# First token chunk of a windowed-attention and SwiGLU kernel: normalising and turning it tile by tile instead of all four tiles together, with the first weight block holding both halves of its unit

## The chip, the cores and the metric

One core of a Trainium2 chip. The metric is device time in microseconds (us). Before the change it is 870.95 us, the median of three runs (868.99 to 872.09).

## The reference

The input is one sequence of 2048 tokens with 512 features. It is normalised without gain or bias; the result feeds both a windowed attention (32 heads of 16, each token sees itself and the 255 before it) and a SwiGLU network with 1792 hidden features. The network's output, passed through another silu, gates the attention's output, and the input is added.

```python
x = A_x
xn = _layernorm(x, axis=-1)             # (x - mean) / sqrt(var + 1e-5)
s = _A_ref(xn, A_wqkv, A_wo)            # q,k,v = xn @ wqkv; window 256; softmax; @ wo
g = _silu(_B_ref(xn, B_w_gate, B_w_up, B_w_down))   # (silu(xn@wg) * (xn@wu)) @ wd
return x + s * g
```

All is float32. A product of two float32 matrices is made here of three products of rounded parts: high with high, high with low and low with high.

## The kernel before, in words

**Tiling.** The tokens are cut into four chunks of 512, a chunk into four tiles of 128. A tile `xt` arrives with tokens on the partitions, is normalised in place, and is turned by TensorE (transposing matmuls against `ident`) into PSUM banks `xp_0` to `xp_3`, one bank for each 128 features, with 512 tokens along it. From each bank ScalarE writes the rounded part `xh`, and VectorE the rest, `xl = xp - xh`. These two are what the matmuls read.

**Weights.** A unit of dense work (`a` for the q and k projections, `g` and `u` for gate and up, `vp`, `d`, `s`) has a weight tile of 128 rows and up to 1024 columns. TensorE is used as two halves of 64 rows that work at the same time: half 0 takes rows 0 to 63 of a unit, half 1 rows 64 to 127, some time later and into the same PSUM bank. Weights therefore travel in blocks: block j holds the lower 64 rows of unit j and the upper 64 rows of unit j-1 (`w_fetch`). A block `wr` is fetched by two DMAs, ScalarE writes its rounded part `wh`, and GpSimd the rest `wl`, in pieces of 512 columns (`w_split`). Unit 0 is `a`, items `a_0` and `a_1`; unit 1 is the first `g` and `u`. So half 0 of `a` reads block 0, and half 1 reads block 1.

**Order.** The whole program is written out by a planner in Python that runs before the chip does anything. It keeps a clock of its own, `now`, and for each engine a queue of operations with a ready time, a slack and an assumed cost (`do`, `dma`); whatever is ready first by these numbers is emitted next. On the chip each engine then takes its instructions strictly in the emitted order and waits on semaphores where data are missing. A wrong assumed cost therefore changes no result, only the order. `next_mm` emits one matmul of one half; `ready` says when a half may go on; due times of the attention's matmuls go by dense work done (`work`), not by time.

**The start.** `load_x(0)` issues the four tile loads, two on SyncE and two on ScalarE. For each tile that lands VectorE runs `stats` (L256 and L257). After the fourth, `first_chain` (L260 to L283) makes the reciprocal root for all four tiles with thirteen small VectorE operations, then VectorE scales the four tiles (L291), and `x_turn` transposes each (L351). After the last tile `x_split` emits the four `xh` (L344) and four `xl` (L335) of 512 tokens. Meanwhile TensorE is given work on a constant tile, `warm_up` (L236): 20 matmuls of 128x128 at the start, 13 that wait for tile 3 to land, and 6 behind the last transposes. The first unit's item 0 takes its twelve 512-column matmuls of half 0 (L463), high parts of `x` first; then half 0 goes on with `a_1`, and half 1 begins `a_0`.

Of the kernel before, what the change touches and what calls it, by code (L numbers as in the profile page):

```python
# [55 lines left out]
def tile_window_attention_swiglu_gate(  # L56
# [181 lines left out]
    def load_x(c):  # L238
# [4 lines left out]
        left = [4]  # L243


        lnb = []
        if c == 0:
            lnb.extend(bank(rb_free, "ln"))
            ve, tm, r1 = (lnb[0][:, 4 * n : 4 * n + 4] for n in range(3))
            hv, t1 = (pers.tile([P, 4], F32, name=n) for n in ("hv", "t1"))  # L250

        def stats(i):
            st = sb(f"st{c}_{i}", [P, 6], F32, "st", 2)
            if c == 0 and i == 3:
                warm_up(xt[c, i][:, :P], 13)
            nc.vector.bn_stats(st, xt[c, i])  # L256
            nc.vector.bn_aggr(mv[:, i, :], st)  # L257

        def eps():
            nc.vector.tensor_scalar(ve, mv[:, :, 1], EPS, None, op0=ALU.add)  # L260

        def root():
            nc.gpsimd.tensor_scalar(ve, mv[:, :, 1], EPS, None, op0=ALU.add)
            nc.gpsimd.tensor_tensor(rs, ve, power[:, :4], op=ALU.pow)
            nc.gpsimd.tensor_tensor(tm, mv[:, :, 0], rs, op=ALU.mult)
            nc.gpsimd.tensor_scalar(tm, tm, -1.0, None, op0=ALU.mult)

        def roots(r=rs):

            i32 = mybir.dt.int32  # L270
            nc.vector.tensor_scalar(tm.bitcast(i32), ve.bitcast(i32), 1, None, op0=ALU.logical_shift_right)
            nc.vector.tensor_scalar(
                r.bitcast(i32), tm.bitcast(i32), -1, 0x5F3759DF, op0=ALU.mult, op1=ALU.add
            )

        def first_chain():
            eps()
            nc.vector.tensor_scalar(hv, ve, -0.5, None, op0=ALU.mult)
            roots(r1)
            for n in range(3):  # L280
                nc.vector.tensor_tensor(t1, r1, hv, op=ALU.mult)
                nc.vector.tensor_tensor(t1, r1, t1, op=ALU.mult)
                nc.vector.scalar_tensor_tensor(rs if n == 2 else r1, t1, 1.5, r1, op0=ALU.add, op1=ALU.mult)  # L283

        def scale(i):
            if c and i % 2 == 0:
                nc.scalar.activation(
                    xt[c, i], xt[c, i], AF.Identity, bias=tm[:, i : i + 1], scale=rs[:, i : i + 1]
                )
                return  # L290
            (nc.gpsimd if c else nc.vector).tensor_scalar(  # L291
                xt[c, i], xt[c, i], mv[:, i, 0:1], rs[:, i : i + 1], op0=ALU.subtract, op1=ALU.mult
            )
# [7 lines left out]

        def after_stats(t):
            left[0] -= 1
            if left[0] == 0 and c:
                do("G", t, 1.9, root, after_newton, sl)
            elif left[0] == 0:
                do("V", t, 2.5, first_chain, after_chain, -1.0)

        def after_chain(t):
            rb_free[lnb[1]] = t  # L310
            after_newton(t)

        def after_newton(t):
            for i in range(4):
                e = "SG"[i % 2] if c else "V"
                do(e, t, {"G": 2.1, "S": 0.62, "V": 0.55}[e], lambda i=i: scale(i), lambda t, i=i: scaled(t, i), sl + 0.3 * i)

# [5 lines left out]
        for i in range(4):  # L323
            dma(now[0], lambda i=i: fetch(i), lambda t, i=i: do("V", t, 0.8, lambda: stats(i), after_stats, sl),
                slack=0.1 * i, can=room(1) if c == 0 else room(5 - i + SPARE), e="S" if c == 0 and i % 2 else "D")

    xhigh = {}
    turned = []

    def x_split(c, k, pb, t, free):  # L330
        hi, lo = (xn[c % 2][s][:, k, :] for s in range(2))

        def low(t):
            xhigh[c, k] = t
            do("V", t, 0.61, lambda: nc.vector.tensor_tensor(lo, pb, f32(hi), op=ALU.subtract), done, -1.0)  # L335

        def done(t):
            free(t)
            xready[c, k] = t
            if k == KC - 1:  # L340
                for i in range(4):
                    give(xt.pop((c, i)))

        do("S", t, 0.52, lambda: nc.scalar.activation(hi, pb, AF.Copy), low, -2.0)  # L344


    def x_turn(i):
        if i == 0:
            turned.extend((bank(p, f"xp0_{k}"), p) for k, p in enumerate((rb_free, rb_free, fb_free, fb_free)))
        for k in range(KC):  # L350
            nc.tensor.matmul(  # L351
                turned[k][0][0][:, i * P : (i + 1) * P], xt[0, i][:, k * P : (k + 1) * P], ident,
                is_transpose=True, start=True, stop=True,
            )
# [16 lines left out]
    def latest(times):  # L371
        times = list(times)
        return None if any(t is None for t in times) else max(times)

    class Unit:
        src = None
        width = 0

        def wts(self, r):
            return wtile[self.n + r]  # L380

# [7 lines left out]
    ended_unit = {}  # L389

    def w_fetch(j):
        lo, up = weighted.get(j), weighted.get(j - 1)
        if lo is None and up is None:
# [4 lines left out]
        def go(r, u):  # L398
            if not box:
                box.append(sb(f"wr{j}", [P, 1024], F32, "wr", 2))  # L400
            move(box[0][half(r), : u.width], u.src[half(r)])
# [6 lines left out]
        for n, (r, u) in enumerate(parts):  # L408
            dma(now[0], lambda r=r, u=u: go(r, u), lambda t, n=n: then(t, n == len(parts) - 1),
                slack=1.0)  # L410

    def w_split(j):
# [3 lines left out]
        t = max(t, ended_unit.get(j - 3, 0.0))  # L416
        w = [weighted[i].width if i in weighted else 0 for i in (j, j - 1)]
        hi, lo = [], []
# [13 lines left out]

        def low(pr, a, b):
            nc.gpsimd.tensor_tensor(lo[0][pr, a:b], raw[pr, a:b], f32(hi[0][pr, a:b]), op=ALU.subtract)  # L434

        def done(t):
            left[0] -= 1
            if left[0] == 0:
                wready[j] = t
                timer(t - 0.5, w_fetch, j + 2)  # L440

        for n, (pr, a, b) in enumerate(cuts):
            sl = (0.0 if j >= 3 else 0.2) + 0.3 * n
            do("S", t, 0.13 + 0.00078 * (b - a), lambda pr=pr, a=a, b=b: high(pr, a, b),
               lambda t, pr=pr, a=a, b=b, sl=sl: do(
                   "G", t, 0.17 + 0.0021 * (b - a), lambda: low(pr, a, b), done, sl), sl)

# [4 lines left out]
    def unit_end(j, t):  # L452
        if (0, j) in half_ended and (j == 0 or (1, j - 1) in half_ended):
            ended_unit[j] = t
            w_split(j + 3)
# [51 lines left out]
    class Stationary(Unit):  # L507
# [11 lines left out]
        def mms(self, i, r, pb):  # L519
            w = [t.rearrange("p (a k n) -> p a k n", a=2, k=KC) for t in self.wts(r)]  # L520
            xs = xn[self.c % 2]
            steps = [(k, a, b) for k in range(KC) for a, b in PAIRS]
            first_unit = self.c == 0 and self.n == 0 and i == 0
            if first_unit:
                steps.sort(key=lambda o: o[2])
            for k, a, b in steps:
                def go(first, last, k=k, a=a, b=b):
                    return mm(pb, w[a][half(r), i, k, :], xs[b][half(r), k, :], first, last)
                if first_unit:
                    yield 512, go, lambda k=k, b=b: (xready if b else xhigh).get((0, k))  # L530
                else:
                    yield 512, go
# [769 lines left out]
    def next_mm(r):  # L1302
# [34 lines left out]
        else:  # L1337
            tag = tags.pop(n)
            if u.src is not None and i == 1:
                half_ended.add((1, u.n))  # L1340
                unit_end(u.n + 1, t)
            u.done(i, banks.pop(n), t, lambda t: fb_free.__setitem__(tag, t))


    def ready(r):
# [8 lines left out]
        if r == 0:  # L1354
            need = [bank_time(fb_free), u.inputs(i)]
            if u.src is not None:
                need.append(wready.get(u.n))
            return latest(need)
# [3 lines left out]
        if u.src is not None:  # L1362
            need.append(wready.get(u.n + 1))
        t = latest(need)
# [5 lines left out]

    xstart = [True]
    load_x(0)
    th0 = pers.tile([P, 1], F32, name="th0")
# [12 lines left out]
    while True:  # L1386
# [84 lines left out]
```

## Time and profile before

| | |
|---|---|
| median of three runs | 870.95 us |
| the profiled execution | 871.37 us |
| its span, first to last instruction | 869.7 us |
| what lies around the span | 1.67 us |
| TensorE busy in the span | 859.5 us (99%) |
| granted TensorE clock, mean | 0.999 |
| last `stats` ends | 8.15 us |
| root ends, scaling begins | 10.6 us |
| last transposes begin | 13.84 us |
| first real matmul (`a_0`, half 0) | 15.77 us |
| `a_1` of half 0 begins | 18.68 us |
| `a_0` of half 1 begins | 19.09 us |

Times inside the span count from its start. In a timeline row the columns are start, length, engine, line, operation, output and inputs, and a count. One 128x128 float32 matmul of the program leaves two records: 20 warm-up matmuls are a row with x40. A row that is merged shows the time from the first record's start to the last one's end. In a table of groups the two numbers behind the bar are the busy time and the mean length of one in ns.

### The profile page before, as it was taken

How to read it: one execution, taken by the hardware profiler on the slowest of the kernel's cores; microseconds unless marked ns; L12 is line 12 of the kernel's file. 1: busy time of each engine (PE TensorE's matmuls, PEld its weight loads, DVE VectorE, ACT ScalarE, POOL GpSimd, SP SyncE). 2: the span in 40 equal slices, each digit the busy share in tenths (PEclk: the TensorE clock that was granted, in tenths of full speed). 3: DMA queues.
4: the chain of work that ended last, by engine and by line, in shares of the span. 5: the costliest groups of instructions: out<-in, count | busy, mean ns of one | idle time of the engine just before them, and what ended most of it. 6: DMA issues, size and time to landing. Idle time of an engine off the chain costs nothing.

```text
span 869.7 us, 30126 instructions
## 1 busy us (share of the span) xinstructions
PE 859.5 (99%) x11966; PEld 798.1 (92%) x11966; DVE 499.1 (57%) x1650; ACT 489.9 (56%) x1046; POOL 627.4 (72%) x871
## 2 busy tenths in 40 slices
PE   9999999999999999999999999999999999999997
PEld 8899889899889998999999999899999999999897
DVE  5364466654765565766576666566555765554234
ACT  3345565555666466655566556655656665666431
POOL 5556587667777778767696798676768688869771
PEclk9999999999999999999999999999999999999999
DMA  5765846567676984766677987546666779644352
GB/s 148 187 167 121 221 115 168 126 162 167 148 198 180 251 201 105 152 156 133 155 184 194 214 200 181 129 145 151 158 150 173 174 187 209 162 130 112 108 126 74
DMA packets 69488, 139.62 MB, mean 161 GB/s; under 512 B 14546, under 2 KB 23250, under 8 KB 69348
## 3 DMA queue, kind: packets, MB, share of 16 engines
q1 hardware_dynamic: 69060, 137.18, 64.1%
q8 instruction: 94, 1.54, 0.8%
q10 hardware_dynamic: 288, 0.52, 0.2%
q14 instruction: 46, 0.38, 0.2%
HBM read 107.74 MB, written 29.62 MB: 158 GB/s over the span
## 4 chain that ended last, share of the span: by engine, by line
PE 93%; DMA 3%; DVE 1%; SPq 1%; POOL 0%; issue 0%; ACT 0%; ACTq 0%; DVEq 0%; POOLq 0%
PE u L463 18%; PE d L463 18%; PE g L463 17%; PE a L463 11%; PE pv L1148 8%; PE s L463 6%; PE c L1111 5%; PE vp L463 5%; PE b L960 4%; DMA q<-ms 1%; DMA r<-rd 1%; DMA xt<-x 1%; SPq L95 1%; DVE xt L291 0%; PE xp L481 0%
## 5 line engine op out<-in xcount | busy, mean ns | idle before, releaser
L434 POOL TENSOR_TENSOR wl<-wr,wh 128x512 fp32r<-128x512 f32 (+3 forms) x258 | 306.8, 1208 | 89.4 <-ACT wh L431 86.9
L968 DVE CUSTOM_DVE_ANT_0 jk<-b,maskb 128x384 bf16<-128x384 f32 (+2 forms) x512 | 271.5, 530 | 130.1 <-PE b L960 64.5
L1072 ACT ACTIVATE p<-c 128x384 f32<-128x384 f32 (+1 forms) x480 | 208.8, 489 | 127.1 <-PE c L1111 106.5
L463 PE MATMUL d<-wh,hh 64*128 64x256 f32 x1792 | 258.2, 278 | 0.0
L463 PEld LDWEIGHTS d<-wh,hh 64*128 64x128 f32 x1792 | 222.9, 185 | 1.0 <-issue 0.6
L463 PE MATMUL d<-wl,hh 64*128 64x256 f32 x896 | 201.3, 277 | 0.0
L431 ACT ACTIVATE wh<-wr 128x512 fp32r<-128x512 f32 (+3 forms) x258 | 142.2, 593 | 51.2 <-PE d L463 11.1
L463 PE MATMUL u<-xh,wh 64*128 64x512 f32 x448 | 167.3, 396 | 0.0
L463 PE MATMUL g<-xh,wh 64*128 64x512 f32 x448 | 167.2, 396 | 0.0
L463 PE MATMUL u<-xl,wh 64*128 64x512 f32 x448 | 166.9, 396 | 0.0
L463 PE MATMUL u<-xh,wl 64*128 64x512 f32 x448 | 166.9, 396 | 0.0
L463 PE MATMUL g<-xl,wh 64*128 64x512 f32 x448 | 166.5, 395 | 0.0
L463 PE MATMUL g<-xh,wl 64*128 64x512 f32 x448 | 164.8, 394 | 0.0
L1085 POOL TENSOR_SCALAR_AFFINE_SELECT p<-p 128x256 f32<-128x256 f32 x256 | 103.7, 410 | 77.1 <-ACT p L1072 75.6
L463 PEld LDWEIGHTS d<-wl,hh 64*128 64x128 f32 x896 | 144.4, 185 | 0.3
L960 PE MATMUL b<-k,q 48*128 48x384 f32 (+1 forms) x512 | 119.2, 333 | 0.0
L1111 PE MATMUL c<-q,k 49*128 49x384 f32 (+1 forms) x704 | 115.5, 302 | 2.3 <-DMA q<-ms 1.2
L1089 POOL TENSOR_SCALAR_AFFINE_SELECT p<-p 128x256 f32<-128x256 f32 x224 | 91.6, 410 | 13.2 <-ACT p L1072 13.1
L463 PE MATMUL a<-xh,wh 64*128 64x512 f32 x256 | 97.2, 394 | 0.0
L463 PE MATMUL a<-xh,wl 64*128 64x512 f32 x256 | 96.4, 392 | 0.0
L616 POOL TENSOR_TENSOR hh<-h,hh 128x512 fp32r<-128x512 f32 x56 | 72.5, 1295 | 33.0 <-ACT hh L612 32.7
L463 PE MATMUL a<-xl,wh 64*128 64x512 f32 x256 | 96.2, 393 | 0.0
(109 smaller groups left out, 2096.6 us busy)
## 6 DMA issues: line engine op xcount, KB each, us to landing
wr<-wgu SPq DMA_DIRECT2D x112, 256.0 KB
k<-qkd SPq DMA_DIRECT2D x48, 192.0 KB
wr<-wqk SPq DMA_DIRECT2D x32, 256.0 KB
qkd<-qkh SPq DMA_DIRECT2D x32, 256.0 KB
qkd<-qkl SPq DMA_DIRECT2D x32, 256.0 KB
q<-qkd SPq DMA_DIRECT2D x64, 128.0 KB
wr<-wdn SPq DMA_DIRECT2D x32, 256.0 KB
od<-ev SPq DMA_DIRECT2D x32, 256.0 KB
```

Source lines behind the costliest of these rows:

```text
L95: eng.dma_start(dst, src)
L431: nc.scalar.activation(hi[0][pr, a:b], raw[pr, a:b], AF.Copy)
L434: nc.gpsimd.tensor_tensor(lo[0][pr, a:b], raw[pr, a:b], f32(hi[0][pr, a:b]), op=ALU.subtract)
L463: return nc.tensor.matmul(pb, a, b, start=first, stop=last, skip_group_check=True)
L616: nc.gpsimd.tensor_tensor(hl[:, 1, :], self.h, f32(hl[:, 0, :]), op=ALU.subtract)
L960: nc.tensor.matmul(pb[:, :w], qs[u % 3][r : r + 48, p, qb * P : (qb + 1) * P], ks[u % 3][r : r + 48, p, lo : lo + w], start=True, stop=True,)
L968: nc.vector.tensor_tensor_reduce(junk[:, :n], pb[:, :n], maskb[:, 3 * P - n :], 1.0, -3.0e38, ALU.add, ALU.max, m[:, col : col + 1],)
L1072: nc.scalar.activation(t[:, h, :], pc[:, a:b], AF.Exp, scale=DH ** -0.5)
L1085: nc.gpsimd.affine_select(s, s, [[0, 2], [1, P]], ALU.is_ge, 0.0, base=0, channel_multiplier=-1)
L1089: nc.gpsimd.affine_select(s, s, [[0, 2], [-1, P]], ALU.is_gt, 0.0, base=0, channel_multiplier=1)
L1111: nc.tensor.matmul(pc[:, at0 : at0 + w], ks[u % 3][r : r + 49, p, k0 : k0 + P], qs[u % 3][r : r + 49, p, qb * P : qb * P + w], start=(i == ...
L1148: nc.tensor.matmul(pbs[r][0][32 * j : 32 * j + 32, q0:q1], vt[half(r), (4 * c + kb) % VT, VW * (4 * g + j) : VW * (4 * g + j) + 32], t[hal ...
```

## The change

Only the first chunk and the first three weight blocks are touched directly.

- Root and scaling go tile by tile. After a tile's `stats`, GpSimd runs `root(i, i + 1)`: add, power, and for the first two tiles also the product `-mean * rs`. The tiles that come first and second are scaled by ScalarE, the third and fourth by VectorE. `first_chain` is gone.
- A tile is turned as soon as it is scaled. When two tiles (256 tokens) are turned, `x_split` emits `xh` and `xl` for that part: eight of each with 256 tokens instead of four with 512.
- Half 0 and half 1 of `a_0` run as 24 matmuls of 256 columns each, in the order high-high, low weights, low `x`, and within each first part 0, then part 1. They may begin when their own part and their own 512 columns of the weight block are there (`wpart`).
- Block 0 holds both halves of unit 0; block 1 holds only the lower half of unit 1; block 2 is as before. `wready` and `unit_end` follow (`block`, `units_of`). Block 2 is fetched at planner time 8.5 into a buffer of its own.
- Block 0's first `wh` piece is pulled ahead (slack -3.0); GpSimd's `wl` waits until all four tiles are normalised, by a one-column copy into `spare`.
- Warm-up: 14 matmuls at the start; then, as long as the start lasts and no tile is ready by the planner's clock, the main loop emits one more and moves its clock on by 0.2133, or by 0.1117 once past 6.9. The 13 and the 6 are gone.

The core of the diff:

```diff
+        def root(a, b):
+            nc.gpsimd.tensor_scalar(ve[:, a:b], mv[:, a:b, 1], EPS, None, op0=ALU.add)
+            nc.gpsimd.tensor_tensor(rs[:, a:b], ve[:, a:b], power[:, a:b], op=ALU.pow)
+            if c == 0 and side(a) == "S":
+                nc.gpsimd.tensor_scalar(
+                    tm[:, a:b], mv[:, a, 0:1], rs[:, a:b], -1.0, op0=ALU.mult, op1=ALU.mult
+                )
...
+        def side(i):
+            return "SG"[i % 2] if c else "SSVV"[came.index(i)]
...
-        if i == 3:
-            warm_up(warm, 6)
-            xstart[0] = False
+        seen.add(i)
+        part = i // 2
+        if {2 * part, 2 * part + 1} <= seen:
             for k in range(KC):
                 (pb, tag), p = turned[k]
-                x_split(0, k, pb, now[0] + 0.2, lambda t, p=p, tag=tag: p.__setitem__(tag, t))
+                x_split(k, part, pb, now[0] + 0.2, lambda t, p=p, tag=tag: p.__setitem__(tag, t))
+        if len(seen) == 4:
+            xstart[0] = False
...
+    def block(n, r):
+        return n + r if n else 0
...
+    def units_of(j):
+        return weighted.get(j), weighted.get(j - 1 if j else 0) if j != 1 else None
...
+            if self.c == 0 and self.n == 0 and i == 0:
+                for a, b in ((0, 0), (1, 0), (0, 1)):
+                    for part in range(2):
+                        n = slice(256 * part, 256 * part + 256)
+                        for k in range(KC):
+                            def go(first, last, k=k, a=a, b=b, n=n):
+                                return mm(pb[:, n], w[a][half(r), i, k, :], xs[b][half(r), k, n], first, last)
...
-    warm_up(warm, 20)
+    warm_up(warm, 14)
...
     timer(7.0, w_fetch, 1)
+    timer(8.5, w_fetch, 2)
...
+        if xstart[0] and now[0] >= 4.1:
+            warm_up(warm, 1)
+            advance(0.2133 if now[0] < 6.9 else 0.1117)
+            continue
```

What the planner makes of it shows in the emitted order. First TensorE at the start, before the change; `xp_k<-ident,xt_i` is the transpose of feature group k of tile i, `[waits ...]` names the engine or DMA lane whose semaphore the instruction waits for.

```order
L236 MATMUL warm<-warm 128x128 x19
L236 MATMUL warm<-xt_3_139,warm 128x128 [waits DMAHW2_49]
L236 MATMUL warm<-xt_3_139,warm 128x128 x12
L351 MATMUL xp_0_206<-ident,xt_0_137 128x128 [waits DVE_49,Pool_49]
...
L351 MATMUL xp_0_206<-ident,xt_3_139 128x128 [waits DVE_49]
...
L351 MATMUL xp_3_209<-ident,xt_3_139 128x128
L236 MATMUL warm<-warm 128x128 x6
L463 MATMUL a_0_244<-xh_79,wh_194 128x512 [waits Activation_49]
```

The same place after the change, from the first matmul to the first ones of `a_1`:

```order
L236 MATMUL warm<-warm 128x128 x36
L338 MATMUL xp_0_191<-ident,xt_1_127 128x128 [waits Activation_49]
...
L236 MATMUL warm<-warm 128x128 x8
L338 MATMUL xp_0_191<-ident,xt_0_129 128x128 [waits Activation_49]
...
L338 MATMUL xp_0_191<-ident,xt_3_131 128x128 [waits DVE_49]
...
L236 MATMUL warm<-warm 128x128
L338 MATMUL xp_0_191<-ident,xt_2_133 128x128 [waits DVE_49,Activation_49]
...
L467 MATMUL a_0_239<-xh_79,wl_220 128x256 [waits Pool_49]
L467 MATMUL a_0_239<-xl_80,wh_219 128x256 [waits DVE_49] x8
L467 MATMUL a_1_284<-xh_79,wh_219 128x512 [waits Activation_49]
```

Before the first transpose stood 20 warm-up matmuls and 13 more; now 37 stand there (one that waits for the constant tile, and the 36 of the row), 8 behind the first tile's transposes and one ahead of the last tile's. The last tile's first transpose now also waits for ScalarE.

Then ScalarE after the change, between its first scaling and the second weight block; `wh` is block 0's rounded part, `xh<-xp_k` a part of 256 tokens.

```order
L268 ACTIVATE xt_1_127<-xt_1_127,tm_92,rs_91 128x512 [waits DMAHW0_49,DVE_49,Pool_49]
L268 ACTIVATE xt_0_129<-xt_0_129,tm_92,rs_91 128x512 [waits DMAHW1_49,DVE_49,Pool_49]
L426 ACTIVATE wh_219<-wr_139 128x512 [waits DMAHW7_49,DMAHW0_49]
L330 ACTIVATE xh_79<-xp_0_191 128x256 [waits PE_49]
L330 ACTIVATE xh_79<-xp_1_192 128x256 [waits PE_49]
...
L330 ACTIVATE xh_79<-xp_0_191 128x256 [waits DVE_49]
...
L330 ACTIVATE xh_79<-xp_3_194 128x256 [waits DVE_49]
L426 ACTIVATE wh_219<-wr_139 128x512
L426 ACTIVATE wh_264<-wr_181 64x512 [waits DMAHW3_49]
```

By the semaphore values, the first `xh` of part 0 waits for tile 3's transpose into `xp_0`, and the other three of part 0 for tile 2's transposes into `xp_1` to `xp_3`; tile 2's first transpose in turn waits for that first `xh` to have read `xp_0`. The `xh` of part 1 wait for the `xl` of part 0 that reads the same bank. The second piece of block 0's `wh` stands behind all eight `xh`.

More of the change, by code (lines that the diff above doesn't have):

```diff
@@ L243, in load_x @@
         left = [4]
[L246 to L250, printed above, removed]
+        came = []
         def stats(i):
+            came.append(i)
             st = sb(f"st{c}_{i}", [P, 6], F32, "st", 2)
-            if c == 0 and i == 3:
-                warm_up(xt[c, i][:, :P], 13)
             nc.vector.bn_stats(st, xt[c, i])
@@ L276, in first_chain @@
[L276 to L283, printed above, removed]
+        def root(a, b):
[5 more added lines that the diff above has]
+                )
+            elif c:
+                nc.gpsimd.tensor_tensor(tm, mv[:, :, 0], rs, op=ALU.mult)
+                nc.gpsimd.tensor_scalar(tm, tm, -1.0, None, op0=ALU.mult)
@@ L433, in low, with done @@
         def low(pr, a, b):
+            if j == 0 and a == 0:
+                nc.gpsimd.tensor_copy(spare, xt[0, list(normed)[-1][1]][:, :1])
             nc.gpsimd.tensor_tensor(lo[0][pr, a:b], raw[pr, a:b], f32(hi[0][pr, a:b]), op=ALU.subtract)
-        def done(t):
+        def done(t, a):
+            wpart[j, a, 1] = t
             left[0] -= 1
@@ L521, in mms, with go @@
             xs = xn[self.c % 2]
[L522 to L531, printed above, removed]
+            if self.c == 0 and self.n == 0 and i == 0:
+                for a, b in ((0, 0), (1, 0), (0, 1)):
+                    for part in range(2):
+                        n = slice(256 * part, 256 * part + 256)
+                        for k in range(KC):
+                            def go(first, last, k=k, a=a, b=b, n=n):
+                                return mm(pb[:, n], w[a][half(r), i, k, :], xs[b][half(r), k, n], first, last)
+                            yield 256, go, lambda k=k, a=a, b=b, part=part: latest(
+                                [(xlow if b else xhigh).get((k, part)), wpart.get((0, 0, a))]
+                            )
+                return
+            for k in range(KC):
+                for a, b in PAIRS:
+                    def go(first, last, k=k, a=a, b=b):
+                        return mm(pb, w[a][half(r), i, k, :], xs[b][half(r), k, :], first, last)
                     yield 512, go
@@ L1362, in ready @@
         if u.src is not None:
-            need.append(wready.get(u.n + 1))
+            need.append(wready.get(block(u.n, 1)))
         t = latest(need)
@@ L1372, in tile_window_attention_swiglu_gate @@
     load_x(0)
+    spare = pers.tile([P, 1], F32, name="spare")
     th0 = pers.tile([P, 1], F32, name="th0")
     timer(1.2, lambda: nc.scalar.activation(th0, warm[:, :1], AF.Tanh))
-    warm_up(warm, 20)
+    warm_up(warm, 14)
     rb_free[wtag] = 14.0
```

93 lines of the change are left out of this document (48 added, 45 removed).

## The prediction

> **What bounds the kernel now.** I read the page first: its busy times and the chain that ended last.
>
> ```profile
> span 869.7 us, 30126 instructions
> PE 859.5 (99%) x11966; PEld 798.1 (92%) x11966; DVE 499.1 (57%) x1650; ACT 489.9 (56%) x1046; POOL 627.4 (72%) x871
> PE 93%; DMA 3%; DVE 1%; SPq 1%; POOL 0%; issue 0%; ACT 0%; ACTq 0%; DVEq 0%; POOLq 0%
> ```
>
> TensorE is the bound nearly everywhere, so a change at the start is worth the time by which the real matmuls start earlier or later, if nothing later eats it. The waits of TensorE over the whole span show what there is to be eaten.
>
> ```profile
> PE c L1111 <- DMA q<-ms: 1.2, 2, 0.6
> PE warm L236 <- DVE warm L231: 1.1, 1, 1.1
> PE c L1111 <- DVE m L968: 1.1, 1, 1.1
> PE mt L994 <- DVE ho L460: 0.9, 1, 0.9
> PE xp L351 <- DVE xt L291: 0.7, 1, 0.7
> PE mt L994 <- DVE m L968: 0.2, 1, 0.2
> ```
>
> Behind the start there are only 3.4 us of it (1.2 + 1.1 + 0.9 + 0.2). Next the timeline of the start.
>
> ```profile
> 1.10 7.52 PE L236 MATMUL warm<-warm 128*128 128x128 f32 x40 [1.10 <-DVE warm L231]
> 5.41 0.18 DVE L257 BATCH_NORM_AGGREGATE mv<-st 128x2 f32<-128x6 f32 x1
> 6.44 0.51 SPq L95 DMA_DIRECT2D wr<-wgu  x1
> 6.99 0.60 SPq L95 DMA_DIRECT2D wr<-wqk  x1
> 7.97 0.18 DVE L257 BATCH_NORM_AGGREGATE mv<-st 128x2 f32<-128x6 f32 x1
> 8.46 3.07 PE L236 MATMUL warm<-xt,warm 128*128 128x128 f32 x26
> 10.44 0.16 DVE L283 SCALAR_TENSOR_TENSOR rs<-t,ln 128x4 f32<-128x4 f32 x1
> 10.64 3.15 DVE L291 TENSOR_SCALAR xt<-xt,mv,rs 128x512 f32<-128x512 f32 x4
> 11.24 1.16 ACT L431 ACTIVATE wh<-wr 128x512 fp32r<-128x512 f32 x2 [2.12 <-DMA wr<-wqk]
> 13.84 0.66 PE L351 MATMUL xp<-ident,xt 128*128 128x128 f32 x4 [0.73 <-DVE xt L291]
> 14.21 2.06 ACT L344 ACTIVATE xh<-xp 128x512 fp32r<-128x512 f32 x4 [1.81 <-PE xp L351]
> 14.33 1.50 PE L236 MATMUL warm<-warm 128*128 128x128 f32 x12
> 15.77 0.49 PE L463 MATMUL a<-xh,wh 64*128 64x512 f32 x1
> 16.10 0.39 PE L463 MATMUL a<-xh,wl 64*128 64x512 f32 x1
> 18.68 0.39 PE L463 MATMUL a<-xh,wh 64*128 64x512 f32 x1
> ```
>
> Today the path is VectorE: statistics until 8.15, the root until 10.60, scaling until 13.79; then transposes and `xh`. The warm-ups fill TensorE's idle time. The row at 18.68 is `a_1` of half 0; half 1 begins three matmuls behind it, before and after the change by the emitted order. From there on the work left is the same in number and kind, so the start of `a_1` is the mark against which I measure.
>
> **The warm-ups, the term that decides.** The change removes the thirteen root operations from VectorE (8.15 to 10.60) and overlaps scaling with statistics. But TensorE works in order, and ahead of the first tile's transposes now stand 37 warm-ups instead of 20 plus 13, with 8 more behind them. What does one cost? Thirteen took 3.07 us and six took 1.50 us: seven more cost 1.57 us, so 0.224 us each, and 0.155 us of tail that the next instruction does not wait for. The code counts 0.1117 us for it, half: that is the pace of a record, and one warm-up leaves two (x26 for 13). At the start they are slower still:
>
> ```profile
> 2.50:6.50 4.00, 4.00 (x21) 4.00 (x20) 0.00 (x0) 0.20 (x1) 1.00 0.91 290
> 8.50:10.50 2.00, 2.00 (x21) 2.00 (x20) 0.00 (x0) 0.00 (x0) 1.00 0.80 195
> ```
>
> These are stretches of the warm tile alone; behind "us" stands TensorE's busy time with its records. As many records take 4 us early and 2 us later, though the granted clock reads 1.00 in both; the step lies near 6.9, since 20 warm-ups need 7.36 us (8.46 - 1.10), which is 12.9 at half pace and 7.1 at full pace. [...]
>
> So the sum: the first 20 stay as they are and end, tail left off, at 8.46. Seventeen more at 0.224 us are 3.81: the first tile can be turned at 12.27. Four transposes take 0.49 us (from 13.84 to the warm-up behind them at 14.33). Then 8 warm-ups (1.79), tile 0's transposes (0.49): tile 3's begin at 15.04. They end at 15.53, one warm-up makes 15.75.
>
> **Are the tiles ready by then?** This is the cover of the new root. Rows of GpSimd, VectorE and ScalarE for the same operations:
>
> ```profile
> L264 POOL TENSOR_TENSOR rs<-ve,power 128x4 f32<-128x4 f32 x3 | 3.2, 1051 | 0.2
> L266 POOL TENSOR_SCALAR tm<-tm 128x4 f32<-128x4 f32 x3 | 0.7, 246 | 0.3
> L263 POOL TENSOR_SCALAR ve<-mv 128x4 f32<-128x4 f32 x3 | 0.7, 232 | 0.3
> L291 DVE TENSOR_SCALAR xt<-xt,mv,rs 128x512 f32<-128x512 f32 x4 | 3.1, 846 | 0.0
> L287 ACT ACTIVATE xt<-xt,tm,rs 128x512 f32<-128x512 f32 x6 | 4.8, 808 | 4.3 <-POOL tm L266 4.2
> ```
>
> The power takes 1.05 us for four columns; for one column no row exists, so it lies between a quarter of that and all of it. I take all, since such small operations are mostly fixed cost (0.23 us for the additions beside it). From 5.59 (first tile's statistics) GpSimd then needs twice 1.53 us and twice 1.28 us: roots at 7.12, 8.65, 9.93 and 11.21. With scaling behind it the tiles are ready at 7.9, 9.5, 10.8 and 12.1. TensorE wants them at 12.27, 14.55, 15.04 and 15.75: all are hidden, with 3 us to spare and more. Block 0, both halves, lands by 11.24 at the latest (so late did a pair issued at 6.44 and 6.99 land, 4.25 us after the second), and ScalarE's wait for it holds up only the `xh` behind it, which cannot begin before 15.4. The copy into `spare` holds GpSimd's `wl` to 12.1, also in time.
>
> **From the transposes to `a_1`.** Here the change adds a wait: tile 2's first transpose waits until ScalarE has read `xp_0`, and behind it on TensorE stand all real matmuls. Parts of 256 have rows in later chunks:
>
> ```profile
> L499 ACT ACTIVATE xh<-xp 128x256 fp32r<-128x256 f32 x24 | 7.8, 387 | 5.1 <-PE xp L481 5.0
> L496 DVE TENSOR_TENSOR xl<-xp,xh 128x256 fp32r<-128x256 f32 x24 | 9.5, 416 | 1.8 <-ACT xh L499 1.8
> L431 ACT ACTIVATE wh<-wr 128x512 fp32r<-128x512 f32 x214 | 126.0, 627 | 45.5 <-PE d L463 10.3 <-PE u L463 8.1 <-PE a L463 5.6
> L434 POOL TENSOR_TENSOR wl<-wr,wh 128x512 fp32r<-128x512 f32 x214 | 273.4, 1294 | 83.9 <-ACT wh L431 82.4 <-PE a L463 1.3
> L434 POOL TENSOR_TENSOR wl<-wr,wh 64x512 fp32r<-64x512 f32 x4 | 5.0, 1275 | 4.8 <-ACT wh L431 4.5 <-POOL xl L896 0.3
> ```
>
> `xh` starts 0.37 us behind a transpose (13.84 to 14.21), so at 15.41, and ends at 15.80; tile 2's transposes begin at 15.85. The second `xh` follows the transpose into `xp_1` (15.97): 16.34. Seven are left. In the row at 14.21 four `xh` of about 0.604 us took 2.06, so neighbours overlap by 0.12 us, and here one starts each 0.268 us: the last begins at 17.95 and ends at 18.34. VectorE's `xl` between them (0.42 each) keep up. Without any overlap the end would be 0.7 us later; that is the upper bound. TensorE takes the last high part at 18.39. Behind it are that one and 16 more of 256 columns, at half the 0.2345 us of a 512-column one (eleven steps from 16.10 to 18.68): 17 x 0.117 = 1.99. So `a_1` begins at 20.38 against 18.68: **1.70 us later**. Block 0's second `wl` is next in line: `wh` to 18.97, `wl` to 20.3, wanted at 20.85 by `a_1`'s third matmul.
>
> Block 1 and 2 land before ScalarE gets to them at 19. Their `wl` (64x512 pieces cost as much as full ones) end by about 22.7 and 25.5, and are wanted around 23.7 and 27: half 0 needs 12 matmuls, 2.8 us, for each item. Block 3's DMA waits for the last reading of block 0's buffer, 20.3, lands some 4.3 us later and is wanted past 30. I cost these at nothing; were block 1 late, it would be by tenths. Splitting 24 matmuls into 48 halves costs nothing in columns.
>
> **The sum.** The profiled execution took 871.37 us, 869.7 of it span; with 1.70 more it is 873.1. That execution is 0.42 us above the median of the runs, so I put the median at 870.95 + 1.70 = 872.65, rounded 872.7. A measurement of this kernel can tell about 0.3% (2.6 us) from no change; so this is no change that shows.
>
> **The rivals.**
>
> *The clock opens earlier.* Each microsecond of half pace costs 0.5 us here (2.2 warm-ups done in it, 4.5 at full pace). [...] For it: nothing in the program ties the moment down. Against: the one trace. [...] Chance 0.15.
>
> *The clock falls back (slower).* From 16.34 to 18.39 TensorE waits for each `xh` and works 8 x 0.117 of 2.05 us, 46%. If that counts as idle, the matmuls behind it run at half pace for as long as at the start, 5.8 us, and lose 2.9: +4.6, 875.6 us. Against:
>
> ```profile
> 12.00:14.00 2.00, 1.27 (x12) 1.03 (x10) 1.79 (x2) 0.40 (x1) 2.00 (x2) 1.00 0.62 180
> ```
>
> at 64% busy nothing fell. It decides if some share between 46% and 64% is the threshold. [...] Chance 0.10.
>
> *The warm-ups are as short as the code counts.* Then the tiles decide: tile 2 is turned at 12.1 instead of 15.85, `a_1` begins at 16.6, 2.0 us earlier than now: 868.9 us. With a power of a quarter of its time VectorE's two scalings set it (8.15 + 1.7), 4.2 us earlier: 866.7 us. Against: x40 records for 20. Chance 0.07.
>
> *The 3.4 us of later waits shrink.* Weights come earlier in relation to TensorE than today, and the attention's places move a little. Half of 3.4 gone makes 871.0 us. But those waits are for `q<-ms` and VectorE, not for weights. Chance 0.11.
>
> **How the numbers follow.** The forecast has 0.57. Its own spread is the overlap of `xh` (+0.7), the moment of the clock, and 1.5 us of the runs' own spread (868.99 to 872.09). Slower by over 0.3% (above 873.6): the falling clock 0.09 and about a fifth of the forecast, 0.13, together 0.22. Faster (below 868.3): half of the short warm-ups 0.035 and stray tails, 0.05. Within: 0.73. The range leaves out the falling clock (0.10), the shortest warm-ups (0.04) and tails (0.06): 869.3 to 875.0.
>
> **What would show it.** In the profile after: x74 records of warm-up from 1.10 to about 12.4; the first `xp` behind them without a wait for ScalarE; tile 2's `xp` waiting a tenth on `xh`; eight `xh` of 0.39 us from 15.4 to 18.3; `a_1` near 20.4. I am wrong if the first `xp` starts before 10, if TensorE waits there for a tile, or if matmuls behind 18 are spaced at twice 0.117 us.

## The result, and the profile after

The changed kernel is slower by more than was forecast. Its median is 877.01 us over five runs (874.59 to 878.59), beside 871.83 us for the kernel before in the same job (868.99 to 872.16). The ratio is 1.0062, with a 95% interval of 1.0037 to 1.0087. Two more sets of it, of twelve runs each on two chips, put it at 1.0031 and 1.0046 (e1 and f1 below). So about 3 to 5 us are lost, where 1.70 were expected.

The head of the changed kernel's page, profiled in an execution of 874.59 us, reads much as before:

```profile
span 872.6 us, 30206 instructions
PE 865.5 (99%) x12004; PEld 803.3 (92%) x12004; DVE 494.7 (57%) x1639; ACT 492.4 (56%) x1052; POOL 632.3 (72%) x882
PE 95%; DMA 3%; DVE 1%; issue 0%; SPq 0%; ACT 0%; POOL 0%; DVEq 0%; ACTq 0%
```

The span grew by 2.9 us (872.6 against 869.7), and TensorE is still the chain. Nothing on this page says why. The timeline of the start does. Its rows for TensorE, with the few of the other engines that make the tiles and the split parts:

```profile
1.11 10.93 PE L236 MATMUL warm<-warm 128*128 128x128 f32 x74 [1.11 <-DVE warm L231]
6.11 0.58 POOL L254 TENSOR_TENSOR rs<-ve,power 128x1 f32<-128x1 f32 x1
10.37 0.55 DVE L272 TENSOR_SCALAR xt<-xt,mv,rs 128x512 f32<-128x512 f32 x1 [0.45 <-POOL rs L254]
11.88 0.60 PE L338 MATMUL xp<-ident,xt 128*128 128x128 f32 x4
...
15.76 2.04 ACT L330 ACTIVATE xh<-xp 128x256 fp32r<-128x256 f32 x7 [0.53 <-PE xp L338]
15.87 2.37 PE L467 MATMUL a<-xh,wh 64*128 64x256 f32 x8
...
19.94 0.63 PE L467 MATMUL a<-xh,wh 64*128 64x512 f32 x1
20.38 0.62 PE L467 MATMUL a<-xl,wh 64*128 64x512 f32 x1
20.80 0.62 PE L467 MATMUL a<-xh,wl 64*128 64x512 f32 x1
```

Read it from the top. The last tile is scaled at 10.92 (10.37 + 0.55), and TensorE is still among its 37 warm-ups; it takes the first transpose at 11.88 without a wait. From 15.76 on an `xh` comes each 0.27 us, and the eight high parts of `a_0` stand spread over them. `a_1` begins at 19.94, 1.26 us later than before. So far it is the forecast's path. The last three rows are not: three matmuls of `a_1` start 0.44 and 0.42 us apart, each 0.62 to 0.63 long, where before they stood 0.2345 apart and the rows were 0.39 long.

The granted clock says what that is. The same execution by stretches; behind TensorE's busy time and its count stand the clock, the DMA share and GB/s:

```profile
16.50:18.50 2.00, 2.00 (x11) 1.00 0.00 0
18.50:20.50 2.00, 2.00 (x17) 0.83 0.00 0
20.50:22.50 2.00, 2.00 (x16) 0.50 0.70 201
22.50:24.50 2.00, 2.00 (x25) 0.81 0.21 61
```

A stretch at 0.83 was at half pace for 0.68 of its 2 us (0.17 of 2 us is missing, and half pace has to last twice as long to lose it), one at 0.81 for 0.76, and the one between for all of it: 3.44 us in all, from 19.82 on. Half pace for so long loses 1.72 us. With the 1.26 that makes 2.98 us, and the span grew by 2.9; that the two agree so closely is partly luck, as the waits below show. In the kernel before the same place reads:

```profile
18.00:20.00 2.00, 2.00 (x14) 1.00 0.23 82
20.00:22.00 2.00, 2.00 (x21) 1.00 0.59 166
```

The waits of TensorE in the changed kernel:

```profile
PE warm L236 <- DVE warm L231: 1.1, 1, 1.1
PE c L1120 <- DMA q<-ms: 0.4, 2, 0.3
PE b L969 <- DMA k<-qkd: 0.3, 1, 0.3
PE c L1120 <- DVE m L977: 0.2, 1, 0.2
PE mt L1003 <- DVE m L977: 0.2, 1, 0.2
```

Behind the start there are now 1.1 us of them instead of 3.4. Had that shortened the span, the loss would have been 2.3 us smaller, so as much went elsewhere in this execution; where is not known. The sum of these waits differs between executions of the same kernel (f1 below has 3.6), so I give it no share.

### The profile page after: what moved, and what is told of

Its sections match the earlier page's. It is cut to its first block, busy times and chain, and to the rows that moved or that the text cites. A ratio compares the mean times of both kernels' runs of the same rounds, so it can differ in the third digit from the quotient of the medians.

```text
span 872.6 us, 30206 instructions
## 1 busy us (share of the span) xinstructions
PE 865.5 (99%) x12004; PEld 803.3 (92%) x12004; DVE 494.7 (57%) x1639; ACT 492.4 (56%) x1052; POOL 632.3 (72%) x882
## 4 chain that ended last, share of the span: by engine, by line
PE 95%; DMA 3%; DVE 1%; issue 0%; SPq 0%; ACT 0%; POOL 0%; DVEq 0%; ACTq 0%
PE u L467 18%; PE d L467 18%; PE g L467 17%; PE a L467 12%; PE pv L1157 8%; PE c L1120 6%; PE s L467 5%; PE vp L467 5%; PE b L969 4%; DMA q<-ms 1%; PE warm L236 1%; DMA wr<-wqk 1%; DMA k<-qkd 0%; PE xp L485 0%; SPq L95 0%
## 5 line engine op out<-in xcount | busy, mean ns | idle before, releaser
L431 POOL TENSOR_TENSOR wl<-wr,wh 128x512 fp32r<-128x512 f32 (+2 forms) x258 | 307.2, 1211 | 88.8 <-ACT wh L426 82.6
L467 PEld LDWEIGHTS d<-wh,hh 64*128 64x128 f32 x1792 | 225.8, 185 | 0.9 <-issue 0.6
L467 PE MATMUL d<-wl,hh 64*128 64x256 f32 x896 | 204.2, 278 | 0.0
L426 ACT ACTIVATE wh<-wr 128x512 fp32r<-128x512 f32 (+2 forms) x258 | 142.1, 594 | 45.7 <-PE d L467 11.1
L467 PEld LDWEIGHTS d<-wl,hh 64*128 64x128 f32 x896 | 147.5, 185 | 0.2
L969 PE MATMUL b<-k,q 48*128 48x384 f32 (+1 forms) x512 | 117.3, 334 | 0.4 <-DMA k<-qkd 0.3
L1098 POOL TENSOR_SCALAR_AFFINE_SELECT p<-p 128x256 f32<-128x256 f32 x224 | 92.5, 414 | 13.4 <-ACT p L1081 11.8
L467 PE MATMUL a<-xh,wh 64*128 64x512 f32 (+1 forms) x264 | 98.6, 397 | 0.0
L467 PE MATMUL a<-xl,wh 64*128 64x512 f32 (+1 forms) x264 | 96.4, 388 | 0.0
L467 PE MATMUL a<-xh,wl 64*128 64x512 f32 (+1 forms) x264 | 96.4, 389 | 0.0
```

Of the source, the lines that this page charges most:

```text
L426: nc.scalar.activation(hi[0][pr, a:b], raw[pr, a:b], AF.Copy)
L467: return nc.tensor.matmul(pb, a, b, start=first, stop=last, skip_group_check=True)
L969: nc.tensor.matmul(pb[:, :w], qs[u % 3][r : r + 48, p, qb * P : (qb + 1) * P], ks[u % 3][r : r + 48, p, lo : lo + w], start=True, stop=True,)
L1098: nc.gpsimd.affine_select(s, s, [[0, 2], [-1, P]], ALU.is_gt, 0.0, base=0, channel_multiplier=1)
```

## The experiments

Theory A says: the warm-ups ahead of the transposes hold them back, and the clock falls because the high parts of `a_0` stand apart. Theory B says that the loss is spread over later chunks. Theory C says that the clock falls because these matmuls use half of the array's rows, not because they stand apart. B' says that the falling clock costs nothing that can be timed. Each kernel was timed beside the kernel before on the same chip; e1 to e4 share one chip, e5 to e8 a second, f1 to f4 a third.

### e1: the changed kernel again

No edit.

> The changed kernel once more, for the spread of its executions. Theory A (the warm-ups delay the transposes by a microsecond or two, and the clock falls to half behind them, each stretch at half pace lasting 3.41 us and costing 1.7 us): 874 to 879 us, the time following the mean granted clock (0.997 to 0.993); the profile shows one or more stretches at 0.50 between 16 and 30 us, and a_1 of half 0 at 19.5 to 20.5. Theory B (the loss is spread over the later chunks, whose order moved): the same 874 to 879, but the profile shows a_1 and the clock as before or no step there, and the loss builds up behind 40 us.

Measured: 874.98 us (873.15 to 878.24) beside 871.30; ratio 1.0031, interval 1.0015 to 1.0046. The granted clock of its twelve executions is 0.994 to 0.997; before's are 0.998 or 0.999 in all but one. This mean counts the whole span, also a fall at its very end that every profile has, the kernel before too (from 867.14 on). In its profile the first transpose stands at 11.61, and the clock falls once more for one stretch. So the falling clock is no accident of one execution.

### e2: the warm-ups counted at their real length

```diff
-    warm_up(warm, 14)
+    warm_up(warm, 7)
...
-            advance(0.2133 if now[0] < 6.9 else 0.1117)
+            advance(0.4266 if now[0] < 6.9 else 0.2234)
```

Ahead of the first transpose now stand 19 warm-ups instead of 37, with 4 and 1 behind.

> The changed kernel with the planner counting a warm-up at its measured price (0.427 and 0.223 us, 7 instead of 14 at the start): 19 warm-ups ahead of the first transpose instead of 37. Theory A: the first transpose at about 8 instead of 11.9, the last tile's at 11.0 instead of 15.3, a_1 of half 0 near 15.7; against the kernel before 3 us less without a fall of the clock (868.8), 1.3 us less with one stretch at half pace (870.5), so 4 us less than the changed kernel. Theory B: the start is earlier, the end is not: within 1 us of the changed kernel, 876 to 877.

Measured: 869.67 us (868.0 to 874.79); ratio 0.9979, interval 0.9959 to 0.9998. The timeline of TensorE:

```profile
1.11 6.68 PE L236 MATMUL warm<-warm 128*128 128x128 f32 x38 [1.11 <-DVE warm L231]
8.04 0.66 PE L338 MATMUL xp<-ident,xt 128*128 128x128 f32 x4 [0.26 <-ACT xt L268]
...
15.57 0.39 PE L467 MATMUL a<-xh,wh 64*128 64x512 f32 x1
...
16.96 0.62 PE L467 MATMUL a<-xl,wh 64*128 64x512 f32 x1
```

The first transpose waits for a tile now, by 0.26 us, so the tiles were ready all along. `a_1` begins at 15.57, 4.37 us earlier than in the changed kernel and 3.11 earlier than before. Behind it the clock still falls, at 15.93 for one stretch (the row at 16.96 is 0.62 long). The loss goes when the start is mended: B falls.

### e3 and e4: the gaps filled with small warm-ups

```diff
+                                if r == 0 and a == b == 0:
+                                    warm_up(warm[:, :64], 1)
                                 return mm(pb[:, n], w[a][half(r), i, k, :], xs[b][half(r), k, n], first, last)
```

e3 is the changed kernel with this; e4 is e2 with this.

> The changed kernel with one 128x64 warm-up ahead of each of the eight high-part matmuls of a_0, which wait for ScalarE 0.27 us apart, so that TensorE stands idle less between 16 and 18 us. Theory A: the clock stays at 1.00 there; a_1 begins within 0.3 us of the changed kernel's, and the time is 1.7 us less per stretch saved: 873 (872 to 874.5), with less spread between executions. Theory B, or a clock that falls for another reason than idle time: no change, 876 to 877.

> Both edits. Theory A: a_1 near 15.8 and no fall of the clock: 3 us less than the kernel before, 868 to 869.5, and the fastest of the four. Theory B: 875 to 877.

Both missed, far to the slow side: e3 took 880.74 us (880.22 to 882.0, four runs), ratio 1.0093 (1.0067 to 1.0119); e4 took 878.20 (875.37 to 881.51, nine runs), ratio 1.0069 (1.0048 to 1.0090). The timeline of e3 shows why:

```profile
16.11 0.43 PE L236 MATMUL warm<-warm 128*128 128x64 f32 x2
16.47 0.38 PE L467 MATMUL a<-xh,wh 64*128 64x256 f32 x1
16.78 0.43 PE L236 MATMUL warm<-warm 128*128 128x64 f32 x2
17.15 0.38 PE L467 MATMUL a<-xh,wh 64*128 64x256 f32 x1
...
25.11 0.62 PE L467 MATMUL a<-xh,wh 64*128 64x512 f32 x1
```

A pair of filler and matmul takes 0.67 to 0.68 us (16.11 to 16.78), and not the 0.27 in which ScalarE delivers: 0.23 us of it is work (0.112, half of a whole warm-up's 0.224, and 0.117 for the 256 columns, an estimate from these prices), and the rest goes between them. The filler is of 128 rows and plain float32, the matmul of 64 rows and of the rounded type, and a pair of one shape and type has no such cost (0.28 us a pair, e5 below); whether the rows or the type make it was not tried. The array then stands idle more than without fillers (an estimated 0.44 of 0.67 us, against 0.17 of 0.28), the clock falls at 19.33 and stays low for three stretches (10.24 us), and `a_1` begins at 25.11. It tells A and C not apart, but it fits the idle part of A: more idling, more half pace.

### e5: each high part made twice

```diff
+                                if r == 0 and a == b == 0:
+                                    mm(wbank[:, n], w[a][half(r), i, k, :], xs[b][half(r), k, n], True, True)
                                 return mm(pb[:, n], w[a][half(r), i, k, :], xs[b][half(r), k, n], first, last)
```

The changed kernel with eight matmuls more, of the same shape, into a bank that nobody reads.

> The changed kernel with each of the eight high-part matmuls of a_0 (half 0) made twice, the first into a spare PSUM bank: extra work of the same shape in the place where TensorE waits for the xh. TensorE is then busy 0.23 of every 0.27 us. Theory A (idle time between 16 and 18 us lets the clock fall): mean granted clock 0.998 to 0.999 as in the kernel before, and about 1.7 to 2 us less than the changed kernel's 875, so 873; a_1 within 0.2 us. Theory C (what lets it fall is that for 4 us only one half of the array works, in short matmuls): clock 0.994 to 0.997 again, 875 or a little more.

Measured: 873.53 us (870.3 to 876.4) beside 871.85; ratio 1.0025, interval 1.0008 to 1.0041. The granted clock of its executions is 0.996 to 0.999 and 0.998 in the mean, as before's on that chip. In its profile no stretch from 12 to 26 is below 1.00, and its timeline has the pairs close together:

```profile
16.17 0.32 PE L467 MATMUL warm<-xh,wh 64*128 64x256 f32 x1
16.33 0.28 PE L467 MATMUL a<-xh,wh 64*128 64x256 f32 x1
16.45 0.32 PE L467 MATMUL warm<-xh,wh 64*128 64x256 f32 x1
```

These matmuls use half of the rows, too, and the clock holds: half of the rows alone does not let it fall, and C as stated falls. That they seem to count beside the gaps comes out further down. By the time alone e1 and e5 can't be told apart, since their intervals overlap and the chips differ; f1 and f2 settle that.

### e6 and e7: high parts and low weights by turns

```diff
-                for a, b in ((0, 0), (1, 0), (0, 1)):
+                for s in (((0, 0), (1, 0)), ((0, 1),)):
...
-                        for k in range(KC):
+                        for k, a, b in [(k, a, b) for k in range(KC) for a, b in s]:
```

Instead of idle work, the low-weight matmul of the same `xh` fills each gap. e6 is the changed kernel with this, e7 is e2 with this.

> The changed kernel with the sixteen high-part matmuls of a_0 in another order: for each part and feature group high weights, then low weights, then the low x parts. The low-weight matmuls, which stood behind, fill the waits. Theory A: a_1 0.9 us earlier (eight times 0.117), and the clock stays up: 2.5 to 3 us less than the changed kernel's 875, 872 to 872.5, level with the kernel before or up to 1 us above. Theory C: 0.9 us less only, clock 0.994 to 0.997.

> The warm-ups counted at their measured price, and the order of the run before: what both findings lead to. Theory A: a_1 near 15.2, clock 0.998 or more; 3 to 4 us less than the kernel before, 867 to 868.5, and under the 869.7 of the same kernel without the new order. Theory C: 868.8, clock below 0.998.

e6: 873.09 us (871.78 to 876.32); ratio 1.0017, interval 1.0002 to 1.0032, a little more than expected. Its windows show no half pace at the start, though no matmul is made for nothing:

```profile
16.00:18.00 2.00, 2.00 (x18) 1.00 0.00 0
18.00:20.00 2.00, 1.75 (x20) 1.00 0.00 0
```

The clocks of its executions, 0.996 to 0.999, leave room for a fall in some. `a_1` did not come 0.9 us earlier: its first matmul stands at 18.85, 7.63 us behind the first transpose (11.22) where the changed kernel has 8.06, so 0.43 us were won. TensorE now waits there for VectorE:

```profile
18.85 0.50 PE L467 MATMUL a<-xh,wh 64*128 64x256 f32 x2 [0.25 <-DVE ho L464]
```

e7: 870.86 (868.03 to 880.89); ratio 1.0003, interval 0.9979 to 1.0027, a miss. Two rows of e7's timeline and its windows tell of the miss:

```profile
11.58 0.38 PE L467 MATMUL a<-xh,wh 64*128 64x256 f32 x1
12.42 0.38 PE L467 MATMUL a<-xh,wl 64*128 64x256 f32 x1 [0.45 <-POOL wl L431]
```

```profile
12.00:14.00 2.00, 1.58 (x13) 1.00 0.59 135
14.00:16.00 2.00, 2.00 (x12) 0.56 0.03 8
16.00:18.00 2.00, 1.75 (x12) 0.50 0.72 182
18.00:20.00 2.00, 2.00 (x19) 0.50 0.32 80
20.00:22.00 2.00, 2.00 (x17) 0.73 0.00 0
```

With the early start GpSimd's `wl` is not there yet; TensorE waits at its second matmul, and the clock falls at 14.25 for 6.83 us (1.76, 2, 2 and 1.08 by these rows).

### e8: early start and doubled high parts

The edits of e2 and e5 together.

> The warm-ups counted at their measured price, and the eight high-part matmuls made twice. Theory A: a_1 as in the run without the doubling (15.6 to 15.8), clock 0.998 or more, 868 to 868.8. Theory C: 869.7 or a little more, clock 0.995 to 0.998.

Measured: 869.40 us (867.32 to 873.87); ratio 0.9970, interval 0.9954 to 0.9986, clock 0.997 to 0.999. It beats the kernel before, and misses the 868 to 868.8 that A expected. A gain of 2.45 us is less than was expected from `a_1`, which begins at 15.53, 3.15 us earlier than before.

### f1 to f4: the four corners on one chip

f1 is the changed kernel, f2 is e5's, f3 is e2's and f4 is e8's, together on a third chip.

> The changed kernel as it is, the first corner of four that stand on one chip: warm-ups counted at half or at their real price, times the high parts of a_0 made once or twice. Theory A (the warm-ups hold the transposes, and the array's clock falls behind the sparse high parts): ratio about 1.003 to 1.005 against before, 2.7 to 4 us, mean granted clock of its executions 0.995 to 0.997. The rival B' (the clock's fall costs nothing that can be timed; the whole loss is the late start) says about 1.0015, which is the 1.26 us by which a_1 came late.

> Second corner: warm-ups as in the change, each high part of a_0's half 0 made twice. Theory A: 1.7 us less than the first corner, ratio 1.001 to 1.0025, clock 0.998. B': the same ratio as the first corner, within 0.5 us.

> Third corner: 19 warm-ups instead of 37 ahead of the first transpose, high parts once. Theory A: a_1 about 4.3 us earlier than in the first corner, the clock still falls (0.997), some tenths go to later waits: 4 to 5 us less than the first corner, ratio 0.998 to 0.9995. B': the same saving, or more.

> Fourth corner: both. Theory A with savings that add: 1.7 less than the third corner, ratio 0.9965 to 0.9975, clock 0.9985. If the later waits take what the clock gives (they rise from 0.5 to 1.5 us for the score matmuls in one trace), about 0.8 us less than the third corner. B': as the third corner.

| | median us (12 runs each) | ratio to before (871.23 us) | median clock |
|---|---|---|---|
| f1: 37 warm-ups, high parts once | 875.25 (873.76 to 878.22) | 1.0046 (1.0028 to 1.0064) | 0.996 |
| f2: 37 warm-ups, high parts twice | 873.49 (871.89 to 875.53) | 1.0018 (0.9999 to 1.0036) | 0.998 |
| f3: 19 warm-ups, high parts once | 869.51 (867.19 to 874.09) | 0.9973 (0.9951 to 0.9995) | 0.995 |
| f4: 19 warm-ups, high parts twice | 870.07 (866.89 to 871.96) | 0.9981 (0.9962 to 1.0001) | 0.998 |

f1 and f2 came as A expected. With the late start, eight matmuls more take 1.76 us off (875.25 - 873.49; between 0.6 and 3.2 when the two sets of runs are resampled), one stretch's price, and B' said at most 0.5. All sets together say the same: among executions of one kernel on one chip, 0.001 less of mean clock goes with 0.8 us more of time (0.6 to 1.0, from 233 executions; one of f1 with 0.966 is left out, since its time shows no such loss), and half pace would give 0.87. So B' falls.

Pricing the warm-ups takes 5.74 us off with the high parts once (f1 to f3) and 3.42 with them twice (f2 to f4). That the two savings add was not seen: from f3 to f4 the clock rises and the time does not fall (+0.56, with 2.2 us more to 2.0 us less when resampled, so 1.7 less is not excluded), and over e2 with f3 and e8 with f4, 24 runs each, the medians are 869.55 and 869.67. Whether the early start gives something back to later waits is not shown: TensorE's waits behind `a_0` in the profile of f4 sum to 1.1 us and in that of f3 to 1.6, and both kernels' executions spread over 5 to 7 us. It stays open.

The profile of f1: the first transpose, `a_1`, and the stretch in which the clock fell.

```profile
12.26 0.60 PE L338 MATMUL xp<-ident,xt 128*128 128x128 f32 x4
...
20.29 0.39 PE L467 MATMUL a<-xh,wh 64*128 64x512 f32 x1
```

```profile
20.00:22.00 2.00, 2.00 (x15) 0.66 0.30 53
22.00:24.00 2.00, 2.00 (x17) 0.50 0.76 209
```

The same place in f2 and the 2 us ahead of it, where nothing falls:

```profile
16.00:18.00 2.00, 2.00 (x17) 1.00 0.00 0
18.00:20.00 2.00, 2.00 (x19) 1.00 0.00 0
20.00:22.00 2.00, 2.00 (x25) 1.00 0.62 176
22.00:24.00 2.00, 2.00 (x23) 1.00 0.32 86
```

In f3 the clock falls for two stretches, and in f4 not at all. f3:

```profile
14.00:16.00 2.00, 2.00 (x15) 0.67 0.03 8
16.00:18.00 2.00, 2.00 (x13) 0.50 0.67 170
18.00:20.00 2.00, 2.00 (x19) 0.50 0.26 92
20.00:22.00 2.00, 2.00 (x17) 0.62 0.00 0
```

## Why the prediction was wrong

**The tiles, right.** The power for one column took 0.58 us (row at 6.11; 0.71 at most), below the 1.05 that was taken for it; the last tile was scaled at 10.92, and TensorE wanted the first at 11.88. All of the new root and scaling lay hidden, as worked out.

**The warm-ups, right.** That they take twice what the code counts, and so decide, is what e2 shows: with half of them the start came 4.37 us earlier. The sum (first transpose 12.27, `a_1` 20.38) gave +1.70; the profiled execution had 11.88 and 19.94, +1.26, and f1's had 12.26 and 20.29, +1.61. What differs is the moment at which full pace begins. From a first transpose at 11.88, 10.77 us less 37 x 0.224 leave 2.48 us lost, so 4.97 us of half pace and an opening at 6.1; f1's is 6.8, e5's (first transpose 11.24) 4.8. The trace's clock records bear it out: they begin with the opening, at 6.18, 6.99 and 4.84, and at 6.98 in the kernel before. (Ahead of its first record the windows read 1.00, which is why the prediction found 1.00 there.) With before's opening, in f1, the sum is right to 0.1 us; only the wait of tile 2's transposes on the first `xh`, a tenth in the sum, did not come. Over the fourteen profiles the records begin between 4.01 and 6.99. So the rival of an earlier opening is partly true in most profiles; it takes some tenths off and leaves the sign. With the clock held, f2 gives what the late start costs in time: 2.26 us (873.49 - 871.23), with an interval from nothing to 3.1.

**The clock, wrong: the step that failed.** "The clock falls back" was a rival with a chance of 0.10, and its loss was in no term of the forecast. In each of the three profiles of the changed kernel it happens, and the clocks of its other executions lie mostly below before's as well. Three parts of that step failed.

- The evidence against it was one row, 64% busy over 2 us without a fall, set beside 46%. Both are shares of time; but the matmuls of that row are of 128 rows, and the high parts of 64. With a matmul of 64 rows counted half, the comparison is 64% against 23%, and the row said little about the latter. By the table below the difference counts: in e7 the clock fell behind a stretch with 13 matmuls of 64 rows and 0.117 us, 76% of two us.
- The rival took 5.8 us of half pace from the start. It was 3.44 us here by the windows (3.413 in the clock records), and twice that in e7 and f3. So the price is 1.7 us a time, not 2.9.
- With the late start added, the rival named +4.6; the same sum with the right length is 1.26 + 1.72 = 2.98 in the profile. In time, e1 has +3.7 (874.98 - 871.30) and f1 +4.0. By the mean clocks of all their executions, 0.0027 and 0.0022 below before's, half pace accounts for 2.4 and 1.9 us of that, and the late `a_1` for 1.26 and 1.61. That e1 and f1 lie near the rival's 875.6 is luck, since its stretch was too long. The first job's +5.2 is above both, and why five runs there were 2 us slower than the others was not tried.

**What decides, by the traces.** In each of the fourteen profiles the rises and falls in the clock records lie whole multiples of 3.413 us apart: in the changed kernel up at 6.18, down at 19.83 (four of them later), up at 23.25. So a span can be cut into windows of that length, counted from the first rise. For each window I add up the array time of its matmuls at the prices above (0.112 us for a record of 128 columns, half of a warm-up's 0.224; 0.117 for 256 columns; 0.2345 for 512), once as it is and once with matmuls of 64 rows counted half. The lowest window at the start of each profile, as an estimate:

| | window from | share of its time | with 64 rows counted half | clock behind it |
|---|---|---|---|---|
| e3, e4 | 15.9, 11.8 | 0.34, 0.34 | 0.25, 0.25 | falls |
| e1 | 15.9 | 0.67 | 0.34 | falls |
| f3 | 11.3 | 0.65 | 0.36 | falls |
| changed kernel | 16.4 | 0.72 | 0.37 | falls |
| e2, f1 | 12.5, 17.2 | 0.78, 0.78 | 0.40, 0.40 | falls |
| e7 | 10.8 | 0.67 | 0.41 | falls |
| e5, e6 | 15.1, 15.1 | 0.84, 0.83 | 0.43, 0.43 | holds |
| f2 | 16.0 | 0.90 | 0.46 | holds |
| e8, f4 | 9.8, 9.6 | 0.74, 0.75 | 0.54, 0.54 | holds |
| kernel before | 10.4 | 0.67 | 0.68 | holds |

The share of time does not sort them: 0.78 fell and 0.67 held. The share with the rows does. Up to 30 us, ahead of the attention, the fourteen profiles have 93 such windows at full pace: the eight with a fall behind them lie at 0.41 or below, the other 85 at 0.43 or above. Behind the attention's last matmul there are 202: the 14 with the fall at the end of the span lie at 0.40 or below, the others at 0.47 or above but one (0.40, in e7). So, by this estimate, the gaps of A and the half rows of C worked together, and the mark lies near 0.42. No run was made to test it. All matmuls of 128 rows here are plain float32 and those of 64 rows in the rounded type, so it could be the type that counts half; and records missing from a trace would move a share by some hundredths.

In the changed kernel the eight high parts start 0.28 us apart (2.37 less the last one's 0.38, by seven), of which 0.17 is waiting (0.28 less 0.117), and the clock fell behind them. The traces of the changed kernel, e1, e2 and f1 show one fall and one return at the start, of 3.4 us each.

**The profile's busy column hid it.** The changed kernel ahead of the fall, by the windows:

```profile
16.00:18.00 2.00, 2.00 (x8) 1.00 0.00 0
```

TensorE reads busy for all of it. The count beside it is what tells: 8 matmuls of 256 columns, where f2 has 17 in the same stretch. A matmul's record is longer than its share of the array (0.27 us and more against 0.117), so records that leave the array waiting still touch.

**The later waits.** They shrank from 3.4 to 1.1 us in the profiled execution, which the forecast had at 0.11 as a gain of half of it. The span shows nothing of it, and f1 has 3.6.

## What to carry to other kernels

Price fillers by their measured length (a warm-up took 0.224 us here at full pace), and in the planner's own clock: half a price nearly doubles them (37 instead of 19), and since TensorE takes them in order, each that is too many delays the work behind it (`a_1` came 4.37 us earlier in e2 with 19). Where a change cuts matmuls into parts that come as another engine delivers them, price the clock as well as the wait: add up the array time over each 3.413 us (the step between rises and falls in these fourteen profiles), with rounded matmuls of half of the rows at half, and where it comes near 0.42 of it or below (an estimate from the table above, not tested), put work of the same shape between them. The second product of the same operand can serve (e6 held 1.00), if its operand is there by then (in e7 it was not: TensorE waited 0.45 us for it, and the clock fell for 6.83). Look at the granted clock behind the place, not at busy time. Add up what two repairs bring only after both were run together.

## What the runs showed of the hardware that was not expected

- A fall of the clock lasts 3.413 us, or two or three times that (6.83 in e7 and f3, 10.24 in e3 and e4), and costs half of its length: matmuls of 512 columns stood 0.42 to 0.44 us apart in it instead of 0.2345, and f2, without the one fall of f1, took 1.76 us less. It begins whole multiples of 3.413 us behind the moment at which full pace began (13.65 us in the changed kernel, e1, e3 and f1).
- That moment differs between executions with the same instructions ahead of it: 4.84, 5.62, 6.18 and 6.99 us, and with it the first transposes, 11.24, 11.61, 11.88 and 12.26 (e5, e1, the first, f1).
- The fourteen profiles sort at 0.41 and 0.43 of a window when rounded matmuls of 64 rows count half of float32 matmuls of 128 (the table above, an estimate that no run tested).
- Float32 matmuls of 128 rows and rounded ones of 64 rows by turns took 0.67 us a pair (e3), while a pair of 64 rows took 0.28 (e5, 16.17 to 16.45), as fast as `xh` came.
- GpSimd's power took 0.58 us for one column and 1.05 for four, so some 0.42 us of it is fixed, an estimate from these two.
